# Gated DeltaNet attention, then a SwiGLU feed-forward block: batch-pair copies, a longer filler for chunk 1, and unread matrix products in the first chain

## The chip, the core and the metric

The kernel runs on one NeuronCore of a Trainium2 chip. The time is the device time of one execution in microseconds (us), the median of several runs; lower is better. TensorE is called PE in the profile (PEld for its weight loads), VectorE DVE, ScalarE ACT, GpSimd POOL and SyncE SP.

## The reference, cut to what matters

Two stages. First a delta-rule attention: for each of 4 batches and 8 heads, a 48 by 48 state is carried over 768 steps. Then all 3,072 tokens (width 384) go through a SwiGLU feed-forward block with an inner width of 1,536.

```python
k_n = k / (norm(k, axis=-1) + 1e-06)
for t in range(768):
    y[:, :, t] = q[:, :, t] @ state                 # read before the update
    v_old = k_n[:, :, t] @ state
    state += beta[t] * outer(k_n[:, :, t], v[:, :, t] - v_old)
x = y.transpose(0, 2, 1, 3).reshape(3072, 384)
g = x @ w_gate
out = (g * sigmoid(g) * (x @ w_val)) @ w_out        # weights arrive as float64
```

## The kernel before, in words

**Chunks.** The 768 steps are cut into 12 chunks of 64. A chunk holds 64 steps of all 4 batches, 256 tokens. Inside a chunk the recurrence is solved as a triangular system. Two chunks form a group, and the inverse of a group's triangular matrix is made on DVE by 31 steps of substitution (`substitute`, two instructions a step, lines 453 and 459: `tmp` and `zb`). `late_z` (486, 492) turns the result into `zt` and `d_t`. `join_late` then puts the two halves of a chunk's inverse together on PE: 32 products `p_j` at line 502, a negating copy on ACT (509), 64 products `p_j` at 517, and four copies into `zt` at 527.

**A chunk's chain** is `advance(c)`, a generator in four steps: (1) `p_r` and `p_y` from the state (not for chunk 0); (2) `p_u` (654) and its copy `uu` (663); (3) the state's products `p_s` (683) and `p_y` (671), with three copies into `y` (702, 704); (4) the transpose `p_f` (714) and the copy `x_ffn` (715). For chunk 0 the state's products come in step 4.

**The feed-forward part** of a chunk is six calls of `gate_val`, each for 256 of the 1,536 inner columns (24 PE passes: `p_gate`, `p_val`; then `sil` on ACT and the product `h_f` on DVE, line 745), and two calls of `output` (12 products `p_o` each). Chunks 0 and 1 are interleaved: three `gate_val` of chunk 0, three of chunk 1, then alternating.

**What sets the order.** Everything stands in program order, written out by hand, in one `manual_schedule`; each engine takes its instructions in that order. Between the PE blocks stand two hooks: `point(c)` emits one step of chunk c's chain or of the preparation of later chunks (`prep_step`: joins, and `products`, the transposes 377 and Gram products 389 of a later chunk's K and Q), and `fill(n)` emits DVE work: first the conversion of the float64 weights to float32 (`convert`, 36 pieces, lines 200 to 250, with an ACT instruction at 208), and when they are done, steps of the next group's inverse (`invert`). `invert` for groups from 2 on first transposes `a_sb` into `mb` (420, 423), then has POOL take a power of its diagonal (544), then scales (551, 553, 554, 323, 438, 440), then substitutes.

**PSUM** is held under four tags: `px` and `py` of two banks each, and `ffn` with four single banks. A tile with a tag waits until the readers of the tile that held it before are done.

**Before the first chunk** the beta values are fetched by 16 small DMAs on POOL's queue (331), K's norms are taken (307, 315 on DVE, 319 on POOL) and `first_betas` (340 to 344, 323) divides by them.

Of the kernel before, what the change touches and what calls it, by code (L numbers as in the profile page):

```python
# [8 lines left out]
FP32 = mybir.dt.float32  # L9
# [5 lines left out]
C = 64  # L15
DP = 64
R = 32
# [4 lines left out]
def kernel(  # L22
# [25 lines left out]
    nc = tc.nc  # L48
# [21 lines left out]
    def ps_pair(name, tag):  # L70

        return psum.tile([128, 2, 512], FP32, name=name, tag=tag, bufs=1)
# [215 lines left out]
    def half_of(x):  # L288
        return slice(64 * x, 64 * x + 64)
# [31 lines left out]
    def divide_beta(g, r_n):  # L321
        for _ in range(2):
            nc.vector.tensor_tensor(
                out=beta_b[:, g], in0=beta_b[:, g], in1=r_n, op=ALU.mult
            )
# [9 lines left out]
            ],  # L335
        )

    def first_betas():
        n = n_t[0].rearrange("p c h -> p (c h)")
        nc.vector.tensor_scalar_add(n, n, 1e-6)  # L340
        r_n = work.tile([128, R], FP32, name="r_n", tag="n_b", bufs=1)
        nc.vector.reciprocal(r_n, n)
        r_b = work.tile([128, R], FP32, name="r_b", tag="nb", bufs=1)
        nc.vector.transpose(r_b, r_n)
        divide_beta(0, r_b)

    def scale_v_heads(c):
        r = vin[c].rearrange("p par bp j d -> p (par bp j) d")
# [8 lines left out]
    def banks(name, tag):  # L357

        if tag == "ffn":
            return [ps_ffn([128, 512], name) for _ in range(2)]  # L360
        p = ps_pair(name, tag)
        return [p[:, 0], p[:, 1]]

    def turned(c, of_q, tag=None):

# [82 lines left out]
    def substitute(mb, zb):  # L448
        for j in range(R - 1):
# [14 lines left out]
            )  # L464
            yield

    QUADS = [(slice(R * n, R * n + R), R * (n % 2)) for n in range(4)]
    z_late = {}

# [22 lines left out]
        nc.vector.transpose(z_late[g], zb)  # L492
        yield

    def join_late(g, c, tags, split=False):

        zt, a, d_t = ztp[g % ZB], a_sb[g], z_late[g]
        p_j = banks("p_j", tags[0])[0].rearrange("p (h i) -> p h i", i=R)
        for h in range(HH):
            for s in range(2):  # L500
                hi, lo = QUADS[2 * s][0], QUADS[2 * s + 1][0]
                nc.tensor.matmul(p_j[hi, h], a[lo, c, h, 0:R], zt[lo, c, h, R:C])  # L502
        t2 = work.tile([128, HH, R], FP32, name="t2", tag="tmp", bufs=1)
        for s in range(2):
            hi = QUADS[2 * s][0]
            if s and split:
                nc.vector.tensor_scalar_mul(t2[hi], p_j[hi], -1.0)
            else:
                nc.scalar.mul(t2[hi], p_j[hi], -1.0)
        yield  # L510
        p_j = [p.rearrange("p (h i) -> p h i", i=C) for p in banks("p_j", tags[1])]
        n_h = HH // 2
        for of_d in (True, False):
            for h in range(HH):
                for s in range(2):
                    hi = QUADS[2 * s][0]
                    nc.tensor.matmul(  # L517
                        p_j[h // n_h][hi, h % n_h, 0:R] if of_d
                        else p_j[h // n_h][hi, h % n_h, R:C],
                        d_t[hi, :, HH * c + h],  # L520
                        ident[hi, hi] if of_d else t2[hi, h],
                    )
        copies = nc.scalar.copy, nc.vector.tensor_copy if split else nc.scalar.copy
        for s, copy in enumerate(copies):
            hi = QUADS[2 * s][0]
            for n in range(2):
                copy(zt[hi, c, n * n_h : (n + 1) * n_h], p_j[n][hi])
        yield

    def invert(g):  # L530
# [84 lines left out]
            )  # L615
        yield

    def recur(p):
        return p[:, :, 0 : NB * NJ * D].rearrange("p x (bp j d) -> p x bp j d", bp=NB, j=NJ)

    def advance(c):

        kn = knp[c % AHEAD]
# [2 lines left out]
        if c > 0:  # L626
            scale_v(c)
        r = vin.pop(c)
        p_y = recur(ps_pair("p_y", "py"))
        if c > 0:  # L630
            p_r = recur(ps_pair("p_r", "px"))
            for bp, j, par, b, first in every():
# [27 lines left out]
                skip_group_check=True,  # L660
            )
        uu = work.tile([128, 2, NB, NJ, D], FP32, name="uu", tag="r", bufs=3)
        nc.scalar.copy(uu, p_u)
        if c + 2 < NCH:
            load_v(c + 2)
        yield
# [30 lines left out]

        if 0 < c < NCH - 1:
            of_state()
        p_of_u()  # L700
        y = work.tile([128, NB, NJ, 2, D], FP32, name="y", tag="r", bufs=3)
        nc.scalar.copy(y[:, :, :, 0], p_y[:, 0])
        for b in range(2):
            nc.scalar.copy(y[half_of(b), :, :, 1], p_y[half_of(1 - b), 1])
        yield

        y_f = y.rearrange("p bp j par d -> p bp (j par d)")
# [3 lines left out]
        for bp in range(NB):  # L711
            for t in range(KT):
                at = slice(t * 128, (t + 1) * 128)
                nc.tensor.transpose(p_f[:, t, bp], y_f[:, bp, at], ident)  # L714
        nc.scalar.copy(xts[c].rearrange("p t (bp n) -> p t bp n", bp=NB), p_f)
        if c == 0:
            of_state()
        yield

    out_v = out.rearrange("(b s) d -> b s d", s=S)  # L720

# [66 lines left out]
    def steps(kind, *args):  # L788
        return gens.get((kind, args), (None, 0))[1]
# [39 lines left out]
    def prep_step(c):  # L829
# [11 lines left out]
        if going:  # L841
            next(going.pop())
            return True
        if not q_of or steps("advance", q_of[0] - 1) < 3:
            return False
        k_c, q_c = None, q_of.pop(0)
        if k_of and steps("advance", k_of[0] - AHEAD) >= 4:
            k_c = k_of.pop(0)
        gen = products(k_c, q_c)
# [45 lines left out]
    with tc.manual_schedule(  # L895
# [9 lines left out]
        for at in range(8):  # L905
            load_beta(at)
        norms(0)
        for at in range(8, 12):
            load_beta(at)

        nc.vector.memset(places[0][:, 0:1], 0)
        norms(1)
        for at in range(12, 16):
            load_beta(at)
        for n in range(4):
            stage(n)
# [8 lines left out]
        stage(11)  # L925
        copy_a, copy_v = nc.scalar.copy, nc.vector.tensor_copy
        turned(0, False)
        gram(0, False)
        turned(1, False, "py")
        gram(1, False, "py", (copy_a, copy_v))  # L930
        mb = new_mb()
        a_v = a_sb[0].rearrange("p c h i -> p i (c h)")
# [6 lines left out]
        for n in range(12, 17):  # L939
            stage(n)  # L940
        load_v(1)
        first_betas()
        zb = scale_m(mb, [(slice(0, R), mb)], beta_b[:, 0])
        nc.gpsimd.memset(ztp[0], 0.0)

# [7 lines left out]
        for n, _ in enumerate(substitute(mb, zb)):  # L953
            if n == R // 2:
                for i in range(4):
                    power_step(i)
        m_1 = turned_m(1, "ffn")
        scale_v_heads(0)
        turned(1, True, "px")
        for _ in late_z(0, zb):  # L960
            pass
        mb = new_mb()
        mbs.append(mb)
        first_join = join_late(0, 0, ("px", "py"))
        next(first_join)
        converts(2)
        next(first_join)
        nc.scalar.copy(mb[:, m_1[0][0]], m_1[0][1])
        next(first_q)
        step("advance", advance, 0)  # L970
        converts(2)
        step("advance", advance, 0)
# [6 lines left out]
        second_inverse.append(invert(1))  # L979
        next(second_inverse[0])  # L980
        second = join_late(0, 1, ("ffn", "py"))
        next(second)
        converts(2)

        def second_join():
            next(second)
            gens["join", (0,)] = [None, 2]
            gram(1, True)

        first.append(second_join)  # L990


        pairs = [(0, 0), (0, 2), (0, 4)] + [(1, 0), (1, 2), (1, 4)]
        pairs += [(c, f) for f in range(6, FT, 2) for c in range(2)]
        for c, f in pairs:
            if c == 1 and f == 0:
                finish(1)
            elif f > 0:
                point(1 if c == 0 and f < 6 else 2)
            need((6, 12, 18, 18, 24, 24)[f // 2])  # L1000
            gate_val(c, f, fill, 1 if c == 0 and f < 6 else None)
        need(len(pieces))
        for bp in range(NB):
            point(2)
            output(0, bp, fill)
        hold.clear()
        for bp in range(NB):
            point(2)
            output(1, bp, fill)
        finish(2)  # L1010
        for c in range(2, NCH):
# [37 lines left out]
```

## Time and profile before

| | us |
|---|---|
| median of 3 runs | 792.59 (791.41 to 794.15) |
| the profiled execution's own time | 788.7 |
| its span, first to last instruction | 786.7 |
| PE busy | 737.0 (94% of the span) |
| DVE busy | 403.8 (51%) |
| ACT busy | 163.6 (21%) |
| POOL busy | 67.9 (9%) |
| mean granted PE clock | 0.964 |

The table is read stage by stage. From about 210 us to the end PE hardly stops; the idle time of PE lies in the first 210 us, and so does the time at a reduced clock. In those first 180 us DVE is busy almost throughout, with the first inverse, the weights' conversion and the second inverse.

### The profile page before, as it was taken

Reading aid. Unit: us, or ns where it says so; the run is one execution under the profiler, and the core shown is the slowest. Engines: PE = TensorE matmul, PEld = TensorE weight load, DVE = VectorE, ACT = ScalarE, POOL = GpSimd, SP = SyncE. Lnnn points to the kernel's source line nnn. Section 1 sums busy time; section 2 is a strip of 40 time slices with the busy share of each in tenths; the row PEclk is TensorE's granted clock in tenths of the full one; section 3 lists DMA queues with packets and bytes.
Section 4 is the critical chain, followed back from the end, with each engine's and each line's share of the span. In section 5 each row is a group of like instructions: output and inputs, shape, how many; then the busy total and the mean of one; then the engine's idle time right before and its main releaser. Section 6 shows DMA issues by size and latency. Waiting matters only on the chain.

```text
span 786.7 us, 21538 instructions
## 1 busy us (share of the span) xinstructions
PE 737.0 (94%) x9800; PEld 588.2 (75%) x9800; DVE 403.8 (51%) x814; ACT 163.6 (21%) x296; POOL 67.9 (9%) x52
## 2 busy tenths in 40 slices
PE   5638899997999999999999999999999999999997
PEld 4537788855788688688688688688688688687784
DVE  5999699994127873067842068832068822021010
ACT  2246243201221211212111112111212111111110
POOL 9106000100003000012000021000020000000000
PEclk9856899998999999999999999999999999999999
DMA  8874244200211200312101112101101000000000
GB/s 149 205 189 116 88 108 137 61 20 12 53 22 23 45 17 3 61 23 42 32 12 19 39 28 43 31 13 23 26 17 22 21 2 2 21 2 1 21 1 20
DMA packets 86683, 34.77 MB, mean 44 GB/s; under 512 B 78848, under 2 KB 81920, under 8 KB 86592
## 3 DMA queue, kind: packets, MB, share of 16 engines
q1 hardware_dynamic: 79872, 27.93, 15.8%
q10 hardware_dynamic: 5952, 5.12, 2.9%
q8 instruction: 77, 1.26, 0.7%
q0 software_dynamic: 768, 0.35, 0.3%
q14 instruction: 14, 0.11, 0.0%
HBM read 28.66 MB, written 4.72 MB: 42 GB/s over the span
## 4 chain that ended last, share of the span: by engine, by line
PE 89%; DVE 5%; ACT 1%; issue 1%; POOL 1%; DMA 1%; ACTq 0%; DVEq 0%
PE p_gate L731 25%; PE p_o L754 24%; PE p_val L731 24%; PE p_g L389 3%; PE p_t L377 2%; PE p_j L517 2%; PE p_u L654 2%; PE p_s L683 2%; PE p_y L671 2%; DVE zb L459 1%; DVE tmp L453 1%; PE p_r L633 1%; PE p_y L642 1%; PE p_f L714 1%; POOL n_t L319 1%
## 5 line engine op out<-in xcount | busy, mean ns | idle before, releaser
L731 PE MATMUL p_gate<-x_ffn,wg_sb 128*128 128x256 f32 x864 | 203.9, 386 | 0.0
L731 PE MATMUL p_val<-x_ffn,wv_sb 128*128 128x256 f32 x864 | 199.3, 381 | 0.0
L754 PE MATMUL p_o<-wo_sb,h_f 128*128 128x384 f32 x576 | 192.4, 491 | 0.0
L731 PEld LDWEIGHTS p_val<-x_ffn,wv_sb 128*128 128x128 f32 x864 | 164.7, 191 | 22.4
L745 DVE TENSOR_TENSOR h_f<-sil,p_val 128x512 f32<-128x512 f32 x72 | 49.3, 685 | 257.1 <-PE p_val L731 256.6
L731 PEld LDWEIGHTS p_gate<-x_ffn,wg_sb 128*128 128x128 f32 x864 | 161.2, 191 | 23.0
L754 PEld LDWEIGHTS p_o<-wo_sb,h_f 128*128 128x128 f32 x576 | 108.7, 192 | 71.8 <-issue 1.4
L740 ACT ACTIVATE sil<-p_gate 128x512 f32<-128x512 f32 x72 | 43.0, 597 | 217.4 <-PE p_gate L731 188.4
L544 POOL TENSOR_TENSOR n_b<-mb,half 128x32 f32<-128x32 f32 x5 | 39.4, 7874 | 441.0 <-DVE mb L423 403.1
L459 DVE TENSOR_TENSOR zb<-zb,tmp 128x31 f32<-128x31 f32 (+15 forms) x186 | 63.7, 343 | 6.4
L453 DVE TENSOR_TENSOR tmp<-zb,mb 128x31 f32<-128x31 f32 (+15 forms) x186 | 63.6, 342 | 5.6
L762 ACT COPY o_sb<-p_o 128x384 f32<-128x384 f32 x24 | 11.5, 478 | 172.0 <-PE p_o L754 165.5
L208 ACT ACTIVATE h_f<-h_f,rebias 128x256 int32<-128x256 uint32 (+2 forms) x36 | 21.0, 612 | 47.0 <-DVE h_f L200 47.0
L692 DVE TENSOR_TENSOR state<-state,p_s 128x768 f32<-128x768 f32 x10 | 9.5, 951 | 26.1 <-PE p_s L683 26.1
L377 PE MATMUL p_t<-ident,kn 128*128 128x128 f32 x96 | 16.8, 324 | 6.5 <-DMA kn<-in_k_dram 5.7
L502 PE MATMUL p_j<-zt,a_sb 32*32 32x32 f32 x256 | 6.2, 214 | 17.3 <-DVE zt L486 11.1
L423 DVE STREAM_TRANSPOSE mb<-a_sb 32x1024 f32<-32x1024 f32 x10 | 21.3, 2135 | 0.3
L377 PEld LDWEIGHTS p_t<-ident,kn 128*128 128x128 f32 x96 | 13.3, 166 | 9.8 <-POOL mask_q L273 4.5
L402 DVE TENSOR_TENSOR p_sb<-p_g,mask_q 128x512 f32<-128x512 f32 x24 | 15.4, 684 | 8.4 <-PE p_g L389 8.4
L389 PEld LDWEIGHTS p_g<-kt 64*64 64x64 f32 x768 | 13.9, 149 | 7.7 <-issue 4.2
L502 PEld LDWEIGHTS p_j<-zt,a_sb 32*32 32x32 f32 x256 | 5.8, 129 | 18.5 <-issue 18.4
L389 PE MATMUL p_g<-kt 64*64 64x64 f32 x768 | 15.5, 236 | 3.7 <-ACT kt L379 2.3
(120 smaller groups left out, 583.9 us busy)
## 6 DMA issues: line engine op xcount, KB each, us to landing
qpad<-in_q_dram SPq DMA_DIRECT2D x48, 96.0 KB, 3.0
vin<-in_v_dram SPq DMA_DIRECT2D x96, 48.0 KB, 2.5
out_dram<-o_sb ACTq DMA_DIRECT2D x48, 96.0 KB, 2.2
kn<-in_k_dram SPq DMA_DIRECT2D x44, 96.0 KB, 3.7
zt<-in_moe_w_out_dram SPq DMA_DIRECT2D x6, 384.0 KB, 3.1
staged<-in_moe_w_out_dram SPq DMA_DIRECT2D x6, 384.0 KB, 3.1
wo_sb<-in_moe_w_gate_dram SPq DMA_DIRECT2D x4, 512.0 KB, 5.5
wo_sb<-in_moe_w_val_dram SPq DMA_DIRECT2D x4, 512.0 KB, 6.9
```

The source lines that it names most:

```text
L208: nc.scalar.activation(power.bitcast(I32), power, ACTF.Relu, bias=rebias, scale=8.0)
L377: nc.tensor.transpose(p_t[bp][:, at], x[:, bp, 2 * j : 2 * j + 2], ident)
L389: nc.tensor.matmul(p_v[par][half_of(b if of_q else b ^ par), bp, j], kt[c][half_of(par), bp, j, b], xt[half_of(par), bp, j, b],)
L423: nc.vector.transpose(out(rows, 0), in_(rows, 0))
L453: nc.vector.tensor_tensor(out=t_v, in0=zb[:, 0 : j + 1, j : j + 1].to_broadcast([128, j + 1, m]), in1=mb[:, j : j + 1, j + 1 : R].to_broad ...
L459: nc.vector.tensor_tensor(out=zb[:, 0 : j + 1, j + 1 : R], in0=zb[:, 0 : j + 1, j + 1 : R], in1=t_v, op=ALU.add,)
L517: nc.tensor.matmul(p_j[h // n_h][hi, h % n_h, 0:R] if of_d else p_j[h // n_h][hi, h % n_h, R:C], d_t[hi, :, HH * c + h], ident[hi, hi] if ...
L544: nc.gpsimd.tensor_tensor(out=n, in0=mb.rearrange("p j i -> p (j i)")[:, 0 : R * R : R + 1], in1=half, op=ALU.pow,)
L731: nc.tensor.matmul(ps[name][:, i], w_sb[:, t, (f + i) * 128 : (f + i + 1) * 128], xts[c][:, t], start=(t == 0), stop=(t == KT - 1),)
L740: nc.scalar.activation(sil, ps[name], ACTF.Silu)
L745: nc.vector.tensor_tensor(out=hs[c, f], in0=sil, in1=ps["p_val"], op=ALU.mult)
L754: nc.tensor.matmul(p_o, hs[c, f - f % 2][:, f % 2, bp * 128 : (bp + 1) * 128], wo_sb[:, f], start=(f == 0), stop=(f == FT - 1),)
```

## The change

1. **The start.** `first_betas` is split: the part that does not need beta (`first_n`: add, reciprocal, transpose) moves ahead of the last Gram copy; only `divide_beta` stays in place. All eight remaining beta DMAs are issued after the second norm's power. K of chunk 1 is transposed before the Gram products of chunk 0.
2. **Batch pairs.** In chunk 0's chain the copies `uu`, `y` and `x_ffn` are made for one pair of batches at a time: two, six and two instructions in place of one, three and one. `join_late` copies into `zt` by batch pairs also (four copies of 512 elements, as before), with its PSUM tile laid out to match.
3. **Unread products.** `keep_awake` issues products of the identity with K of chunk 0 whose result nothing reads: five of 128x512 in the gap of the first inverse (released by a memset on DVE, ten steps before the substitution's end), one of 128x512 between the two halves of the first join, one of 128x512 ahead of `p_u`, one of 128x256 ahead of `p_y` and one of 128x512 ahead of `p_f`.
4. **The order of chunks 0 and 1.** Four `gate_val` of chunk 0, then four of chunk 1, then alternating. Chunk 0's first `gate_val` no longer waits behind the state's products and the second join; these become hooks inside it. K of chunk 4 may be prepared without a Q; so K of chunk 4 is transposed during chunk 0's third `gate_val`, and K of chunk 5 goes with Q of chunk 2 during chunk 1's first two. The hook ahead of chunk 1's first `output` is dropped.

The line numbers of the changed kernel are higher by 8 to 30.

```diff
-    def first_betas():
+    def first_n():
         ...
         nc.vector.transpose(r_b, r_n)
-        divide_beta(0, r_b)
+        return r_b
...
+    def keep_awake(p, n):
+        moving = knp[0].rearrange("p bp h d -> p (bp h d)")
+        for i in range(n):
+            nc.tensor.matmul(p, ident, moving[:, 0 : p.shape[-1]], start=True, stop=True)
...
-    def join_late(g, c, tags, split=False):
+    def join_late(g, c, tags, split=False, awake=False):
...
+        p_j = ps_pair("p_j", tags[1])
+        if awake:
+            keep_awake(p_j[:, 0], 1)
...
-            for n in range(2):
-                copy(zt[hi, c, n * n_h : (n + 1) * n_h], p_j[n][hi])
+        for bp in range(NB):
+            for s, copy in enumerate(copies):
+                hi = QUADS[2 * s][0]
+                copy(
+                    zt_v[hi, :, bp].rearrange("p par j i -> p par (j i)"),
+                    p_j[hi, :, bp].rearrange("p par j i -> p par (j i)"),
+                )
...
-        p_y = recur(ps_pair("p_y", "py"))
+        p_y2 = ps_pair("p_y", "py")
+        if c == 0:
+            keep_awake(p_y2[:, 0], 1)
+        p_y = recur(p_y2)
...
-        nc.scalar.copy(uu, p_u)
+        each = range(NB) if c == 0 else (slice(0, NB),)
+        for bp in each:
+            nc.scalar.copy(uu[:, :, bp], p_u[:, :, bp])
...
+        if c == 0:
+            keep_awake(p_y2[:, 0, 0:256], 1)
         p_of_u()
+        if c == 0:
+            keep_awake(ps_pair("p_w", "px")[:, 0], 1)
...
-        nc.scalar.copy(y[:, :, :, 0], p_y[:, 0])
-        for b in range(2):
-            nc.scalar.copy(y[half_of(b), :, :, 1], p_y[half_of(1 - b), 1])
+        for bp in each:
+            nc.scalar.copy(y[:, bp, :, 0], p_y[:, 0, bp])
+            for b in range(2):
+                nc.scalar.copy(y[half_of(b), bp, :, 1], p_y[half_of(1 - b), 1, bp])
...
-        nc.scalar.copy(xts[c].rearrange("p t (bp n) -> p t bp n", bp=NB), p_f)
+        for bp in each:
+            nc.scalar.copy(x_v[:, :, bp], p_f[:, :, bp])
+        yield
         if c == 0:
             of_state()
-        yield
+            yield
...
-        if not q_of or steps("advance", q_of[0] - 1) < 3:
+        if q_of and steps("advance", q_of[0] - 1) >= 3:
+            q_c = q_of.pop(0)
+        elif not (hold and k_of and steps("advance", k_of[0] - AHEAD) >= 4):
             return False
...
         turned(0, False)
+        turned(1, False, "py")
         gram(0, False)
-        turned(1, False, "py")
+        r_b = first_n()
         gram(1, False, "py", (copy_a, copy_v))
...
+            if n == R - 11:
+                nc.vector.memset(awake, 0.0)
...
+        p_w = ps_pair("p_w", "py")
+        nc.tensor.matmul(p_w[0:1, 1, 0:1], awake, ident[:, 0:1], start=True, stop=True)
+        keep_awake(p_w[:, 0], 5)
...
-        next(second)
         converts(2)
+        def state_and_join():
+            step("advance", advance, 0)
+            next(second)
...
-            gram(1, True)
-        first.append(second_join)
+        first.extend((state_and_join, second_join, lambda: gram(1, True)))
...
-        pairs = [(0, 0), (0, 2), (0, 4)] + [(1, 0), (1, 2), (1, 4)]
-        pairs += [(c, f) for f in range(6, FT, 2) for c in range(2)]
+        pairs = [(c, f) for c in range(2) for f in range(0, 8, 2)]
+        pairs += [(c, f) for f in range(8, FT, 2) for c in range(2)]
...
         for bp in range(NB):
-            point(2)
+            if bp > 0:
+                point(2)
             output(1, bp, fill)
```

## The prediction, made before the changed kernel ran

> **What bounds the kernel now.** I read the page's engine shares first, then the chain that ended last, PE's waits, the granted clock in 1 us windows, and last the timelines of DVE, ACT and POOL.
>
> ```profile
> PE 737.0 (94%) x9800; PEld 588.2 (75%) x9800; DVE 403.8 (51%) x814; ACT 163.6 (21%) x296; POOL 67.9 (9%) x52
> PEclk9856899998999999999999999999999999999999
> ```
>
> PE is the bound, at full clock from about 220 us on. What an edit can win lies in the first 210 us: PE's idle time and its cold time. PE's waits name the idle:
>
> ```profile
> PE p_j L502 <- DVE zt L486: 11.1, 1, 11.1
> PE p_j L502 <- issue: 6.2, 1, 6.2
> PE p_g L389 <- ACT zt L527: 2.2, 1, 2.2
> ```
>
> The first is the first inverse on DVE. The second is put down to "issue", but the chain shows DVE's second inverse, whose `zt` ends at 182.34:
>
> ```profile
> 155.60 20.64 PE p_o L754 x64
> 176.24 6.20 issue
> 182.44 1.92 PE p_j L502 x64
> ```
>
> The granted clock in 1 us windows, the third figure from the right:
>
> ```profile
> 33.00:34.00 1.00, 0.72 (x52) 0.64 (x45) 0.93 (x3) 0.00 (x0) 0.00 (x0) 0.89 0.18 29
> 71.00:72.00 1.00, 1.00 (x58) 0.91 (x52) 1.00 (x5) 0.46 (x1) 1.00 (x1) 0.83 0.73 246
> 78.00:79.00 1.00, 1.00 (x41) 1.00 (x37) 0.00 (x0) 0.00 (x0) 1.00 (x1) 0.58 0.92 320
> 84.00:85.00 1.00, 1.00 (x4) 0.82 (x3) 0.72 (x2) 0.00 (x0) 0.00 (x0) 0.51 0.00 0
> ```
>
> It is 0.5 or 1.0, so each mean gives the instant: down at 33.78, up at 71.34, down at 78.16, up at 84.98. The steps are 11, 2 and 2 times 3.41 us. At 78.16 it fell although PE was 100% busy: with 32x32 products (`p_j`, 75.39 to 79.18), and 0.65 us of full-size ones before them.
>
> **What the Trainium skill says.** "TensorE: Matmul & The Clock Gate", Part 1: the clock is halved after an idle window of 3,413 ns and restored after a busy one, the windows running freely. The trace agrees, and adds that small products count as idle. The same page, Part 1 (architectural detail) and Part 3: ACT and DVE take instructions strictly in order, and matmuls never pass each other; so an unread product delays all behind it. "ScalarE: Activation LUTs", what ACT_TABLE_LOAD costs: an ACTIVATE has a fixed part (186 ns) and 0.833 ns an element. Here 384 elements take 0.48 and 768 take 0.80: 0.83 ns an element and 0.16 fixed. So 192 elements cost 0.33 (estimate), and halving a copy adds about 0.16.
>
> **The change, part by part** (after minus before, us).
>
> *Start: -0.65.* L340, L342 and L344 with their gaps (23.75 to 24.59) leave the path to the substitution: -0.84. They wait for POOL's second power, now directly behind the first (12.71+2.95=15.66); the last Gram copy queued behind them starts at 16.5, not 16.1, which the beta wait (0.35) nearly hides: +0.1. The eight beta DMAs behind the powers end at the same 20.1. The memset: +0.1.
>
> *The five products: 0 on the path.* PE idles 11.05 us there. Released near 44.1, at 1.72 us cold (a 128x256 product is 2 passes of 0.216 warm, so 512 is 0.86 warm), they wake the clock within two windows and end before 52.
>
> *First join and chunk 0's chain: +0.75.*
> - `p_j` L502 warm: 1.75 to 1.20: -0.55.
> - The product between the halves: +0.86.
> - L517: before 2.86 (with a 1.0 us hole) and 2.05, cold; warm it takes 1.9 a half anyway. I keep half the hole: -0.65.
> - Ahead of `p_u`: the product waits until all four `zt` copies have released `py`, and `p_u` stands behind it. Between the last product and this one lie 6.2 us of L517 and idling, more than any window in which the clock survived (75.39 to 81.38: it fell). So I take it that the clock falls once more near 58 to 61 and is back about 63: product 1.66 and `p_u` 1.85 on average, against 1.95 + 0.05: +1.5. Ends: 2.0 if warm, 4.2 if cold throughout.
> - `uu` to `p_y`: 0.81 + 2.0 before; 0.48 and 1.05 after, the 256 product hidden: -1.3. The first `uu` copy waits for all of `p_u`, so only the copy is halved.
> - `y`: on ACT stand `mb` L973 (0.59) and two L208 (0.92) ahead of it. Before, 0.79 of idling followed them; now PE is ahead of ACT and waits 0.8. Then six copies of 0.33 for three of 0.49: +1.3. `p_f` needs all six; the product ahead of it is hidden.
> - `p_f` warm: -0.67. `x_ffn`, two copies, 1.0, stood beside `p_s` and `p_j` (3.02, cold); now PE waits for it, then does those two in 2.25: +0.25.
>
> Sum -0.55+0.86-0.65+1.5-1.3+1.3-0.67+0.25 = +0.74.
>
> *Second join: -3.1.* Before, after L517:
>
> ```profile
> 79.20 1.05 ACT zt L527 x2
> 80.27 1.07 ACT zt L527 x2
> 81.38 1.99 PE p_g L389 x64
> 83.37 3.62 PE p_val L731 x12
> ```
>
> A `p_gate` now covers the 2.2 us; with `p_g` at 1.05 and `p_val` at 2.6 this is -4.15. L517's 3.8 us still stand alone between feed-forward products: a window fits into it in some 6 of 10 phases, and costs 1.7: +1.0.
>
> *Chunk 1's chain: +3.1.* Two waits before (`vin` 0.71, `uu` 0.33) go: -1.0. New ones, following each engine's queue: Gram of chunk 4 behind its `kt` copies, behind an L208: 0.35; `p_u` for `vin` (L355, L650 queued behind a conversion): 0.65; and steps 3 and 4 now come in `finish(1)` with no filler: `y` behind an L208 0.7 and its copies 1.5, `x_ffn` 0.9. Sum +4.1. Before, three `gate_val` covered these, the last one the copies. Chunk 5's transposes and Grams (1.84) come here from 225 to 234 us: nothing in the sum. Its K, issued on SP behind eight `vin` loads, lands near 113.5 and is needed at 115: hidden, up to 1.6 if it took the slowest K load's 6.1.
>
> *Up to the second inverse: -0.8.* Its release is the last `h_f`, which waited behind L440 (155.33 to 156.47); DVE is ahead now.
>
> *Chunk 5 early: +3.5.* Group 2's inverse starts as soon as K of 5 is there, so DVE's queue after `d_t` holds: `mb` transposes (2.13, 4.2), the wait for POOL's power, the scaling, two steps, and only then `vin` L355 and L650, for which `p_u` of chunk 2 waits. The same work later in the trace of before:
>
> ```profile
> 240.63 2.16 DVE L423 STREAM_TRANSPOSE mb<-a_sb 32x1024 f32<-32x1024 f32 x1
> ...
> 249.12 0.90 DVE L551 TENSOR_SCALAR n_b<-n_b 128x32 f32<-128x32 f32 x1 [4.27 <-POOL n_b L544]
> ...
> 251.35 1.23 DVE L440 TENSOR_TENSOR mb<-mb,nb 128x1024 f32<-128x1024 f32 x1
> ```
>
> From the transposes' end to L440's end: 9.8. Counted from the start of `p_j`: transposes end at +8.2, L440 at +18.0, steps 1.0, `vin` 2.05: +21.05. PE arrives at +17.6 (`p_j` 1.92, `p_o` 4.3, L517 3.75, `p_o` 2.78, `p_r` and `p_y` 2.0, `p_o` 2.78). So 3.5 of new waiting.
>
> *Dropped hook:* it emitted nothing on PE's path; 0. Afterwards PE has the same work as before: 0.
>
> Sum: -0.65+0.74-3.1+3.1-0.8+3.5 = **+2.8**. On the profiled execution 788.7 becomes 791.5; that one lies 3.9 below the median of the runs, so on the median it is 792.6 + 2.8 = **795.4**. A measurement tells some 0.3% (2.4 us) from no change, so this is just slower.
>
> **The rivals.**
> 1. *The clock holds (same).* If one product of 0.86 in a window is enough and the second L517 falls well, the +1.5 becomes 0 and the +1.0 goes: 2.8-2.5 = +0.3, 792.9. For it: it survived 187.4 to 190.8 with 1.26 us of `p_o` in the window. Against: it fell with 0.65, and from 54 to 60.5 there is nothing full-size.
> 2. *Faster.* The clock holds and `p_u` of chunk 2 does not wait: 0.3-3.5 = -3.2, 789.4. Its place is DVE's queue at the second inverse; it decides if POOL's 6.21 us power starts over 3.5 us earlier against PE, or PE is later. For it: PE would be later by as much as a cold clock adds. Against: the order of both queues is fixed.
> 3. *The unread products don't wake the clock (slower).* Then the first join and chain run cold: `p_j` +0.55, the product ahead of L517 +0.86, `p_u` and its product +0.7, `p_y` +0.9, `p_f` +0.7, less what ACT's queue hides, about +3: 798.4. Against: full-size products for 8 us.
>
> **How the numbers follow.** Forecast 0.42; rival 1 0.32, rival 2 0.18, rival 3 0.08. The first is slower by over 0.3% in most of its width (K of chunk 5 late, the hole in L517 0 to 1 us, clock phase 1.7), and so is rival 3; rival 1 is within. Slower 0.48, same 0.32, faster 0.20. The range 788.8 to 798.6 takes in rival 2 and most of rival 3; the slower forecast's own is 793.5 to 798.
>
> **What would show it.** Right: full clock at 52 us, half clock near 60; the `y` copies starting after L208; PE waiting about 2.5 us around `p_f` of chunk 1; `p_u` of chunk 2 waiting 3.5 us for DVE `vin`; the `p_j` of the second inverse near 182 to 184. Wrong: full clock without a break from 50 to 110 us, or no wait at that `p_u`.

## The result, and the profile after

| | before | after |
|---|---|---|
| median, us | 793.37 (791.41 to 794.15) | 797.75 (796.99 to 799.78) |
| ratio, 95% interval | 1 | 1.0063 [1.0034, 1.0092] |
| the profiled execution's own time, us | 788.7 | 798.41 |
| its span, us | 786.7 | 796.3 |

The changed kernel is slower by 0.6%, 2.4 us above the forecast of 795.4 and inside its range. The two profiled executions are 9.7 us apart, the medians 4.4; why they differ is told at the end of the next section.

The page of the changed kernel, engine shares and granted clock:

```profile
PE 748.4 (94%) x9820; PEld 590.8 (74%) x9820; DVE 403.9 (51%) x815; ACT 164.0 (21%) x301; POOL 66.3 (8%) x52
...
PEclk9677989998979999999999999999999999999999
```

PE is busy 11.4 us longer, which is about what the unread products take: 6.13 in the gap of the first inverse and 5.53 in the chain. PE's waits (total, times, longest):

```profile
PE p_j L514 <- issue: 6.2, 1, 6.2
...
PE p_f L739 <- ACT y L729: 5.0, 3, 2.3
...
PE p_u L672 <- DVE vin L668: 3.3, 2, 2.6
...
PE p_j L514 <- DVE zt L498: 1.7, 1, 1.7
```

The gap of the first inverse is filled (11.1 us of waiting became 1.7 at `p_j` and 2.7 at the releasing product). The 6.2 us ahead of the second inverse's `p_j` stayed to the tenth, but it stands elsewhere: that `p_j` starts at 189.69, where it was 182.44. DVE releases it, so the next question is what held DVE back. Its waits from the first join's `p_j` to this one, before:

```profile
DVE p_sb L402 <- PE p_g L389: 6.2, 1, 6.2
DVE h_f L745 <- PE p_val L731: 3.8, 3, 2.4
DVE h_f L241 <- ACT h_f L208: 0.4, 1, 0.4
```

and after:

```profile
DVE h_f L773 <- PE p_val L759: 18.3, 7, 7.3
```

DVE waits 7.9 us longer, and its second inverse is about that much later, less the 0.5 us by which it began earlier (first substitution step at 26.07, before 26.59). All of the waits after are for PE's `p_val`. DVE's timeline shows where the longest of them lies:

```profile
111.79 0.95 DVE L712 TENSOR_TENSOR state<-state,p_s 128x768 f32<-128x768 f32 x1
112.66 0.42 DVE L220 TENSOR_SCALAR wg_sb<-staged 128x512 uint32<-128x512 uint32 x1
...
114.71 0.69 DVE L250 SCALAR_TENSOR_TENSOR wg_sb<-wg_sb,h_f 128x512 f32<-128x512 f32 x1
122.75 0.69 DVE L773 TENSOR_TENSOR h_f<-sil,p_val 128x512 f32<-128x512 f32 x1 [7.35 <-PE p_val L759]
```

After one weight conversion (112.66 to 115.4) the next instruction in DVE's queue is the first `h_f` of chunk 1, whose `p_val` ends only at 122.7. Before, the last steps of chunk 1's chain had three `gate_val` around them, each of which hands DVE conversions; now they stand in `finish(1)`, which hands it none. PE's timeline for the same stretch:

```profile
109.25 1.11 PE L691 MATMUL p_y<-uu,p_sb 64*64 64x48 f32 x64
112.69 1.54 PE L739 MATMUL p_f<-ident,y 128*128 128x128 f32 x6 [2.33 <-ACT y L729]
115.12 4.93 PE L759 MATMUL p_gate<-x_ffn,wg_sb 128*128 128x256 f32 x12 [0.89 <-ACT x_ffn L742]
119.89 2.75 PE L759 MATMUL p_val<-x_ffn,wv_sb 128*128 128x256 f32 x12
```

The two waits were forecast (2.2 and 0.9). What came with them was not: PE's clock falls there. The windows (third figure from the right is the clock) give 112.52 and 119.36, two steps of 3.41 us apart (down, then up again):

```profile
112.00:113.00 1.00, 0.31 (x2) 0.31 (x3) 1.00 (x2) 0.63 (x2) 0.00 (x0) 0.76 0.11 15
119.00:120.00 1.00, 1.00 (x5) 0.83 (x5) 0.00 (x0) 0.00 (x0) 0.00 (x0) 0.82 0.00 0
```

`p_gate` takes 4.93 instead of 2.86 and `p_f` 1.54 instead of 0.87: 2.7 us, all of it inside DVE's wait.

**Which engine leads.** That DVE waits does not yet make it the bound: it waits for PE. Look at the tenth `gate_val` of the two chunks, before (PE, then the `h_f` on DVE):

```profile
142.49 2.75 PE L731 MATMUL p_val<-x_ffn,wv_sb 128*128 128x256 f32 x12
...
155.44 20.80 PE L754 MATMUL p_o<-wo_sb,h_f 128*128 128x384 f32 x64
182.44 1.92 PE L502 MATMUL p_j<-zt,a_sb 32*32 32x32 f32 x64 [6.20 <-issue]
```

```profile
145.35 0.69 DVE L745 TENSOR_TENSOR h_f<-sil,p_val 128x512 f32<-128x512 f32 x1
```

and after:

```profile
149.76 2.75 PE L759 MATMUL p_val<-x_ffn,wv_sb 128*128 128x256 f32 x12
...
162.71 20.80 PE L782 MATMUL p_o<-wo_sb,h_f 128*128 128x384 f32 x64
189.69 1.92 PE L514 MATMUL p_j<-zt,a_sb 32*32 32x32 f32 x64 [6.18 <-issue]
```

```profile
152.62 0.69 DVE L773 TENSOR_TENSOR h_f<-sil,p_val 128x512 f32<-128x512 f32 x1
```

In both, `h_f` starts 0.11 us after its `p_val` ends (145.24 and 152.51), with DVE free for 0.1 us before it, too short to be listed as a wait. In the changed kernel each of the first ten `h_f` starts so; before, eight of the twelve do. PE meanwhile has no wait that the profile lists: in the changed kernel from chunk 1's `x_ffn` on, in the kernel before from 97 us on. So PE's path, with its own waits for ACT and DVE, leads up to the tenth `gate_val`. From there DVE has 37.1 us of work of its own up to `p_j`, in both kernels, and `p_j` stands 27.0 us behind the start of PE's `p_o`, in both. What moved is PE's arrival at `p_o`: 162.71 instead of 155.44, +7.27. DVE's longer waits are how it follows.

PE's account to `p_o`: it starts 0.52 earlier at the first `p_j`; from there it idles 10.18 us instead of 7.58 (+2.6), the unread products take 5.5, and K of chunk 5 (transposes and Gram products) some 2.0. The remaining -2.3 goes with the clock, which is halved for 17.1 us of this stretch instead of 25.4.

The other place where time is lost is behind the second inverse:

```profile
209.72 1.15 PE L672 MATMUL p_u<-vin,zt 64*64 64x48 f32 x64 [2.59 <-DVE vin L668]
...
217.35 0.87 PE L739 MATMUL p_f<-ident,y 128*128 128x128 f32 x6 [1.69 <-ACT y L729]
218.16 1.82 PE L514 MATMUL p_j<-zt,a_sb 32*32 32x32 f32 x64
219.90 5.44 PE L759 MATMUL p_gate<-x_ffn,wg_sb 128*128 128x256 f32 x12
```

The span splits without a rest at two landmarks, the second inverse's `p_j` and chunk 2's second `p_gate` (218.60 before, 231.62 after). Up to the first: +7.25. Between them: 41.93 instead of 36.16, so +5.77 (`p_u`'s wait 2.59, colder `p_j` 0.62 and `p_gate` 2.58). From the second to the end: 564.68 instead of 568.10, so -3.42: K of chunk 5 is missing here (its work, 1.84 us in the prediction's count, now stands in the first part), and the 1.6 us wait at the `p_f` of chunk 4 is gone. Sum +9.6, the difference of the spans.

### The profile page after: what moved, and what is told of

It is laid out like the page before. It is cut to its first block, busy times and chain, and to the rows that moved or that the text cites. A ratio compares the mean times of both kernels' runs of the same rounds, so it can differ in the third digit from the quotient of the medians.

```text
span 796.3 us, 21574 instructions
## 1 busy us (share of the span) xinstructions
PE 748.4 (94%) x9820; PEld 590.8 (74%) x9820; DVE 403.9 (51%) x815; ACT 164.0 (21%) x301; POOL 66.3 (8%) x52
## 4 chain that ended last, share of the span: by engine, by line
PE 83%; DVE 11%; POOL 2%; ACT 1%; issue 1%; DMA 1%; ACTq 0%; DVEq 0%
PE p_gate L759 24%; PE p_val L759 23%; PE p_o L782 20%; DVE zb L467 3%; DVE tmp L461 3%; PE p_g L397 2%; PE p_t L385 2%; PE p_u L672 2%; PE p_j L532 1%; PE p_y L691 1%; PE p_s L703 1%; PE p_r L651 1%; PE p_f L739 1%; PE p_y L660 1%; POOL n_t L319 1%
## 5 line engine op out<-in xcount | busy, mean ns | idle before, releaser
L759 PE MATMUL p_gate<-x_ffn,wg_sb 128*128 128x256 f32 x864 | 209.2, 393 | 1.8 <-ACT x_ffn L742 1.8
L759 PEld LDWEIGHTS p_gate<-x_ffn,wg_sb 128*128 128x128 f32 x864 | 163.7, 195 | 26.0 <-ACT x_ffn L742 2.5
L461 DVE TENSOR_TENSOR tmp<-zb,mb 128x31 f32<-128x31 f32 (+15 forms) x186 | 63.5, 342 | 15.9 <-PE p_j L532 10.4
L562 POOL TENSOR_TENSOR n_b<-mb,half 128x32 f32<-128x32 f32 x5 | 37.8, 7563 | 378.8 <-DVE mb L431 337.6
L668 DVE TENSOR_TENSOR vin<-vin,p_r 128x768 f32<-128x768 f32 x11 | 10.5, 954 | 23.9 <-PE p_r L651 23.0
L672 PEld LDWEIGHTS p_u<-vin,zt 64*64 64x64 f32 x768 | 13.1, 142 | 8.8 <-DVE vin L668 4.3
L385 PE MATMUL p_t<-ident,qpad 128*128 128x128 f32 x96 | 14.5, 298 | 5.2 <-DMA qpad<-in_q_dram 5.2
L683 ACT COPY uu<-p_u 128x768 f32<-128x768 f32 (+1 forms) x13 | 9.6, 749 | 40.0 <-PE p_u L672 40.0
L672 PE MATMUL p_u<-vin,zt 64*64 64x48 f32 x768 | 14.6, 227 | 3.3 <-DVE vin L668 3.3
```

The lines of the kernel that those rows point to most:

```text
L385: nc.tensor.transpose(p_t[bp][:, at], x[:, bp, 2 * j : 2 * j + 2], ident)
L461: nc.vector.tensor_tensor(out=t_v, in0=zb[:, 0 : j + 1, j : j + 1].to_broadcast([128, j + 1, m]), in1=mb[:, j : j + 1, j + 1 : R].to_broad ...
L562: nc.gpsimd.tensor_tensor(out=n, in0=mb.rearrange("p j i -> p (j i)")[:, 0 : R * R : R + 1], in1=half, op=ALU.pow,)
L672: nc.tensor.matmul(p_u[half_of(b), par, bp, j], zt[half_of(b ^ par), par, bp, j], r[half_of(b ^ par), par, bp, j], start=first, stop=True, ...
L759: nc.tensor.matmul(ps[name][:, i], w_sb[:, t, (f + i) * 128 : (f + i + 1) * 128], xts[c][:, t], start=(t == 0), stop=(t == KT - 1),)
```

## The experiments

Theory A: until the second inverse DVE is the bound, and its idle time counts one to one. The rivals: B, the unread products and halved copies cost; C, PE's own path decides, as the prediction summed it, and what DVE has in its queue does not matter. D, later, concerns the early K of chunk 5. To tell A from C, two numbers are read in each trace: when PE starts `p_o`, and how far the second `p_j` stands behind that. If DVE's queue matters, the second one changes. Every ratio is to the kernel before on the same chip, with its 95% interval.

**Part 4, the order, alone**, on the kernel before.

```diff
-        pairs = [(0, 0), (0, 2), (0, 4)] + [(1, 0), (1, 2), (1, 4)]
-        pairs += [(c, f) for f in range(6, FT, 2) for c in range(2)]
+        pairs = [(c, f) for c in range(2) for f in range(0, 8, 2)]
+        pairs += [(c, f) for f in range(8, FT, 2) for c in range(2)]
...
+        first.extend((state_and_join, second_join, lambda: gram(1, True)))
```

> The kernel before with part 4 of the change alone (four gate_val of chunk 0, then four of chunk 1; K of chunks 4 and 5 early; second join inside chunk 0's first gate_val); start, single copies and no unread products as before. Theory A (the loss is made by the new order: the last steps of chunk 1's chain stand with no gate_val and no conversion beside them, DVE idles there, and its second inverse, which PE waits for near 190 us, comes later): slower than before, 797 to 803 us, ratio 1.005 to 1.012, with a DVE wait of 5 to 8 us at the first h_f of chunk 1 and the p_j of the second inverse at 189 to 194 us. Theory B (the loss is made by the unread products and the halved copies in chunk 0's chain): within 0.3% of before. Theory C (the sum in the prediction, PE's path): terms of the order alone are -3.1+3.1-0.8+3.5=+2.7, so 796.

Measured 797.52, ratio 1.0073 [1.0050, 1.0096]; DVE waits 6.10 at the first `h_f` of chunk 1, `p_j` at 189.72. The order alone makes the whole loss, so B is out as its cause; between A and C the time does not tell, as both forecast about this. PE starts `p_o` at 162.76, and `p_j` comes 27.0 us later, as before.

**The rest without part 4.**

```diff
-        pairs = [(c, f) for c in range(2) for f in range(0, 8, 2)]
-        pairs += [(c, f) for f in range(8, FT, 2) for c in range(2)]
+        pairs = [(0, 0), (0, 2), (0, 4)] + [(1, 0), (1, 2), (1, 4)]
+        pairs += [(c, f) for f in range(6, FT, 2) for c in range(2)]
```

> The changed kernel with part 4 taken back: the order of gate_val and hooks as before, but the new start, the batch pairs and the unread products kept. Theory A (the order makes the loss): as before or a little faster, 789 to 793.5 us, ratio 0.995 to 1.000; DVE's waits up to the second inverse at most the 10.4 us of before. Theory B (unread products and halved copies make it): as the changed kernel, 796 to 799, ratio 1.004 to 1.007. Theory C (the prediction's sum): -0.65+0.74=+0.1, so 793.4, ratio 1.000.

Measured 792.01, ratio 1.0015 [1.0001, 1.0028]: start, batch pairs and unread products bring nothing that can be told. In this execution the first `p_j` comes 1.6 us earlier (51.20 instead of 52.79), but PE starts `p_o` at 155.32, practically where it did before: the chain with its 5.0 us of unread products takes the start back. DVE waits 13.0 us, so A's forecast of at most 10.4 was wrong.

**Without the unread products.**

```diff
-        if awake:
-            keep_awake(p_j[:, 0], 1)
...
-        keep_awake(p_w[:, 0], 5)
```

> The changed kernel without any unread product (the five in the gap and the four in chunk 0's chain left out, with the memset and the small product that release them); nothing that is read is left out. Theory A: chunk 0's chain runs at the halved clock, its first feed-forward block comes 1 to 3 us later, DVE waits as much longer for the first h_f, and the end comes up to 3 us later than with them: 798 to 801, ratio 1.005 to 1.010. Theory B (the unread products cost more than they bring): faster than the changed kernel by their own time on the path (some 3 us): 794 to 795, ratio 1.001 to 1.003.

Measured 797.26, ratio 1.0072 [1.0048, 1.0097], against 1.0063 with them: neither gain nor cost. Chunk 0's chain runs cold (`p_f` 1.54, first `p_gate` 5.46), but from the first `p_j` to its first `p_val` 25.36 us pass (53.11 to 78.47), where the changed kernel takes 25.45 (52.27 to 77.72): what the products win in clock they spend themselves. DVE's waits are the same to 0.1 us (18.4).

**Three conversions moved into chunk 1's last steps.** PE's work stays, DVE gets something to do: A and C forecast different times.

```diff
             while steps("advance", c) < 4:
                 step("advance", advance, c)
+                if c == 1:
+                    converts(2 if steps("advance", 1) < 4 else 1)
```

> The changed kernel with three of the 36 weight conversions moved forward on DVE: two are issued after the third step and one after the fourth step of chunk 1's chain, where DVE waits 7.35 us for the first h_f of chunk 1 in the changed kernel. PE's order and work stay. Theory A (DVE's idle time there sets when the second inverse ends): that wait falls below 1.5 us, the p_j of the second inverse comes 5 to 7 us earlier (183 to 185 us instead of 189.7), and the time is 791 to 793.5, ratio 0.997 to 1.000. Theory C (PE's own waits and cold clock in that place make the loss, as the prediction's sum has it): PE's work before 190 us is the same and its waits too, so no change: 797 to 798.5, ratio 1.005 to 1.007.

Measured 803.02, ratio 1.0153 [1.0126, 1.0179]: slower, against both theories. The trace has a part of A's forecast: `p_j` comes at 186.19, 3.5 us earlier, though PE starts `p_o` 2.3 us later (165.02); from there to `p_j` it is 21.2 us instead of 27.0. Then 45.64 us pass to chunk 2's second `p_gate` instead of 41.93. Two suspects: `x_ffn` on ACT behind the conversions' activations (PE waits 3.20 instead of 0.89), or DVE's queue after the inverse. So the conversions were put behind `x_ffn`:

```diff
+                if c == 1:
+                    converts(3) if steps("advance", 1) == 4 else None
```

> The changed kernel with three weight conversions moved forward on DVE to the end of chunk 1's chain, behind x_ffn; K of chunk 5 early as in the change. It tells why the first such version, with the conversions ahead of x_ffn, was slower (803). If the x_ffn copy, 2.3 us late behind them on ACT, was the reason: 792 to 794, ratio 0.999 to 1.003. If the reason is DVE's queue at the second inverse (the scaling of the inverse of chunks 4 and 5, which waits 4.8 us for POOL, then stands ahead of the zt copies of chunk 2's join, for which PE waits): 799 to 803, ratio 1.009 to 1.015, with PE waiting 2 to 4 us for DVE zt.

Measured 801.89, ratio 1.0126 [1.0095, 1.0157]. The wait for `x_ffn` is back at 0.89, and the kernel is still slow: mainly the queue, then. DVE's timeline of this kernel, and then PE's:

```profile
193.43 0.69 DVE L519 TENSOR_SCALAR t<-p_j 32x512 f32<-32x512 f32 x1
198.95 0.90 DVE L569 TENSOR_SCALAR n_b<-n_b 128x32 f32<-128x32 f32 x1 [4.83 <-POOL n_b L562]
...
203.50 0.69 DVE L542 COPY zt<-p_j 32x512 f32<-32x512 f32 x1
```

```profile
198.88 1.15 PE L651 MATMUL p_r<-state,kt 64*64 64x48 f32 x64
205.67 1.96 PE L660 MATMUL p_y<-state,qt 64*64 64x48 f32 x64 [5.64 <-DVE zt L542]
```

In the changed kernel the `zt` copies stand ahead of this wait for POOL (200.27 and 203.25); here they stand behind it. As the conversions end sooner, the inverse of chunks 4 and 5 is issued earlier. The early K of chunk 5 lets it start there at all, so K was made late:

```diff
-        elif not (hold and k_of and steps("advance", k_of[0] - AHEAD) >= 4):
+        elif not (hold and k_of and k_of[0] == AHEAD and steps("advance", k_of[0] - AHEAD) >= 4):
...
-        if k_of and steps("advance", k_of[0] - AHEAD) >= 4:
+        if k_of and (k_of[0] - AHEAD < 1 or q_c != 2) and steps("advance", k_of[0] - AHEAD) >= 4:
```

> The changed kernel with K of chunk 5 prepared as late as before (with Q of chunk 3 instead of Q of chunk 2), so that the inverse of chunks 4 and 5 no longer starts while chunk 2's chain runs; K of chunk 4 stays early. By the prediction's step 'chunk 5 early' (wait for vin, 2.6 us in the trace of the changed kernel, with the clock that falls behind it): the p_u of chunk 2 waits under 1 us, and the time is 2.5 to 4 us shorter, 794 to 795.5, ratio 1.001 to 1.003. If that queue on DVE costs nothing because another wait takes its place: 797 to 798.5.

Alone, measured 797.84, ratio 1.0078 [1.0053, 1.0103]: no gain, though the wait at `p_u` of chunk 2 is gone. From the second landmark to the end it has 567.8 us again, not 564.7: what the late K saves at `p_u` it gives back there.

**Both: conversions moved, K of chunk 5 late.**

> The changed kernel with K of chunk 5 late, and with three weight conversions moved forward on DVE to the end of chunk 1's chain (behind x_ffn on ACT, so that x_ffn is not delayed, as it was by 2.3 us where they stood ahead of it). Theory A (DVE's idle time ahead of the second inverse makes most of the loss, the early inverse of chunks 4 and 5 the rest): second inverse's p_j 5 us earlier than in the changed kernel, at 183 to 186, nothing on DVE ahead of its zt copies, 790 to 793, ratio 0.998 to 1.001. Theory C (PE's own waits and cold clock make it): no better than with K of chunk 5 late alone, 794 to 796.

Measured 792.83, ratio 1.0010 [0.9989, 1.0031], `p_j` at 183.20. Against the same kernel without the moved conversions this is 5.0 us in the medians, with PE's products as they were. PE starts `p_o` 1.9 us later than there (162.01, was 160.09) and still `p_j` comes 4.25 us earlier: it follows `p_o` by 21.2 us instead of 27.4. So DVE's queue matters, and C as it was put is out. Nor does A hold one to one: DVE's wait at the first `h_f` of chunk 1 fell from 7.37 to 0.14, by more than `p_j` moved. What the moved conversions shorten is DVE's work behind the last `h_f` that PE releases: that is now the twelfth, and only 20.9 us of work follow it, where in the changed kernel 37.1 us followed the tenth. The other 1.8 us of the 6.1 us between the two spans lie behind `p_j`. The queue at the second inverse was the reason that the first test failed.

**Four more unread products in chunk 1's last two steps**, on the changed kernel.

```diff
+        if c == 1:
+            keep_awake(ps_ffn([128, 512], "p_w"), 3)
         y_f = y.rearrange("p bp j par d -> p bp (j par d)")
...
+        if c == 1:
+            keep_awake(ps_ffn([128, 512], "p_w"), 1)
         x_v = xts[c].rearrange("p t (bp n) -> p t bp n", bp=NB)
```

> The changed kernel with four more unread 128x512 products in chunk 1's last two steps: three ahead of its p_f, where PE waits 2.3 us, and one ahead of the x_ffn wait, so that PE's clock does not fall there (it falls at 112.5 us in the changed kernel: p_f 1.54 instead of 0.87, the p_gate behind it 4.93 instead of 2.86). If that cold spell is on the path, through DVE's wait for the first h_f of chunk 1 or through PE: 2 to 3 us shorter, 795 to 796, ratio 1.002 to 1.004. If it is hidden (PE waits 6 us for the second inverse anyway, and DVE is not moved): 797.5 to 798.5.

Measured 796.25, ratio 1.0048 [1.0033, 1.0064]. The clock stays up, and from `p_s` to `p_val` 9.09 us pass instead of 11.61. But in the profiled execution that chain had begun 2.6 us later, so PE starts `p_o` where it did (162.78), and the second `p_j` stands where it was (189.76). The time is between the two forecasts, and its interval overlaps that of the changed kernel: the cold spell's price in time stays open.

**The inverse of chunks 4 and 5 held** until `p_u` of chunk 2 is issued; K of chunk 5 early.

```diff
-            if fills:
+            if fills and (fills[0][0] != 2 or steps("advance", 2) >= 2):
```

> The changed kernel with K of chunk 5 prepared early as it is, but DVE's inverse of chunks 4 and 5 held back until p_u of chunk 2 is issued, so that it no longer stands ahead of vin. With K of chunk 5 late, the wait of that p_u went, yet the time did not: theory D says that the early K of chunk 5 also gives back as much as the wait costs (its 1.84 us of PE work is done before the second inverse, where PE idles 6.2 us, and fills a 1.6 us wait at p_f of chunk 4). Then holding the inverse alone keeps the gain and drops the wait: 794 to 795.5, ratio 1.002 to 1.0045. If the wait at p_u only moves on to the next release: 797 to 798.5.

Measured 796.10, ratio 1.0060 [1.0038, 1.0083], above the forecast. The wait at `p_u` is gone, and the last part stays short (564.4). So D is seen in the trace, but a gain in time from holding the inverse alone can't be told from the changed kernel's 1.0063.

**The kernel before with two conversions moved** into its own 6.2 us wait.

```diff
         next(second)
         converts(2)
+        converts(2)
```

> The kernel before with two of the 36 weight conversions moved forward on DVE, into its 6.2 us wait for the second join (ahead of p_sb). PE's work stays as it is; as the conversions end sooner, the second inverse's join is issued one block of products earlier. Theory A (up to the second inverse DVE is the bound, and its idle time counts one to one): DVE's waits fall from 10.4 to some 6 us, the second inverse's p_j comes 4 to 5 us earlier (178 instead of 182.4), and the kernel is 3 to 5 us faster than before, ratio 0.994 to 0.997. Theory C (PE's path decides): within 0.3% of before.

Measured 791.00, ratio 0.9982 [0.9966, 0.9997]: just outside no change, and much less than forecast. `p_sb` waits 2.7 instead of 6.2, and the first `h_f` 3.57 instead of 2.36, as PE reached it 2.9 us later (`h_f` at 89.94 instead of 87.08): PE's wait for the join's copies on ACT grew from 2.2 to 3.7. DVE's waits sum to 10.8, `p_j` is at 181.75. This is where the two numbers are plainest: `p_j` follows `p_o` by 23.4 us instead of 27.0, but PE starts `p_o` 2.9 us later (158.30), and 0.7 us is left.

**A version from these runs**: the changed kernel with three conversions at the end of chunk 1's chain, the inverse of chunks 4 and 5 held, and the four products.

> The changed kernel with three edits that the runs point to: three weight conversions moved forward to the end of chunk 1's chain, the inverse of chunks 4 and 5 held until p_u of chunk 2, and four unread products in chunk 1's last two steps that keep PE's clock up. By theory A and D their gains add (about 5.4, 3 and 1.5 us, the first and last partly the same DVE wait): second inverse's p_j at 180 to 184 us, 788 to 791, ratio 0.994 to 0.998. If the gains share one wait: 792 to 794.

Measured 788.35, ratio 0.9962 [0.9947, 0.9976], `p_j` at 181.47. With the clock up in chunk 1's chain PE starts `p_o` at 160.29, 2.4 us earlier than in the changed kernel, and `p_j` follows by 21.2. And with two more conversions ahead of chunk 0's first `gate_val`:

```diff
         second = join_late(0, 1, ("ffn", "py"))
         converts(2)
+        converts(2)
```

> As the kernel with the three edits, and two more conversions moved forward, to ahead of chunk 0's first gate_val, where DVE waits 4.5 us for the first h_f. Theory A: 2 to 4 us faster still, 785 to 789, ratio 0.991 to 0.996. Against it: their ACT instructions stand ahead of the state copy and of the join's copies on ACT, as in the kernel before with two conversions moved, where a part of DVE's wait only moved on to the next h_f; then no better than without this edit.

Measured 782.67, ratio **0.9883 [0.9852, 0.9914]**, faster than both kernels and than was forecast. DVE's waits in this kernel between the two `p_j` (another, of 0.2, is left out):

```profile
DVE h_f L777 <- PE p_val L763: 6.0, 6, 1.8
DVE h_f L200 <- DMA staged<-in_moe_w_out_dram: 1.7, 1, 1.7
DVE h_f L200 <- DMA zt<-in_moe_w_out_dram: 0.9, 1, 0.9
```

And PE's timeline at the join:

```profile
171.68 8.23 PE L786 MATMUL p_o<-wo_sb,h_f 128*128 128x384 f32 x25
179.84 1.20 PE L514 MATMUL p_j<-zt,a_sb 32*32 32x32 f32 x64
180.97 2.85 PE L786 MATMUL p_o<-wo_sb,h_f 128*128 128x384 f32 x8
```

There is no idle time ahead of `p_j` any more: PE comes last, 18.2 us after `p_o` began. The clock, which in the kernel with three edits fell in that idle time (at 180.87), stays up, and `p_j` takes 1.20, not 1.92. That is why it won more than its 1.6 us of earlier `p_j` over that kernel (781.4 to 785.9 in the spans): the part behind it takes 36.99 instead of 39.76.

**The runs by the three parts.** From the first join's `p_j` to the start of PE's `p_o`; from there to the second inverse's `p_j`; DVE's waits in these two together, and what is left of them without the waits; then from that `p_j` to chunk 2's second `p_gate`; then to the end (us, one profiled execution each).

| kernel | PE to `p_o` | on to the second `p_j` | DVE's waits | rest | to `p_gate` | to the end |
|---|---|---|---|---|---|---|
| before | 102.7 | 27.0 | 10.4 | 119.3 | 36.16 | 568.1 |
| after | 110.4 | 27.0 | 18.3 | 119.1 | 41.93 | 564.7 |
| order alone | 110.4 | 27.0 | 18.3 | 119.1 | 42.82 | 563.5 |
| without the order | 104.1 | 27.8 | 13.0 | 118.9 | 39.02 | 568.0 |
| without unread products | 110.5 | 27.0 | 18.4 | 119.1 | 40.28 | 564.3 |
| K of 5 late | 108.5 | 27.4 | 16.9 | 118.9 | 38.01 | 567.8 |
| conversions behind `x_ffn` | 112.7 | 21.2 | 15.8 | 118.1 | 46.65 | 567.7 |
| the same, K of 5 late | 109.5 | 21.2 | 12.5 | 118.2 | 35.64 | 568.4 |
| two conversions, before | 105.9 | 23.4 | 10.8 | 118.5 | 40.05 | 568.3 |
| three edits | 107.9 | 21.2 | 11.1 | 118.0 | 39.76 | 564.7 |
| and two conversions more | 109.1 | 18.2 | 8.8 | 118.4 | 36.99 | 564.6 |

The rest column is an account and not a cause: DVE has the same work in every kernel (118 to 119 us, in the three kernels not listed too), so its waits must make up any difference, whoever causes it. The first two columns tell who does. Where no conversion is moved, the second one is 27.0 (up to 27.8 in the two kernels where DVE had waited 0.5 to 0.9 us for a DMA), and the whole loss stands in the first, PE's. Where conversions are moved, the second one falls to between 18.2 and 23.4; what they win there, less what PE's arrival loses, is the gain at `p_j`. Which part of the new order costs PE how much was tested only for K of chunk 5 (2.0 us to `p_o`); what the steps without a filler cost (waits of 2.33 and 0.89 us, and the clock that falls there) is read from the traces, not tested by itself.

The column to `p_gate` holds the luck: the kernel without part 4 has the order of before there, and takes 39.02 where before took 36.16, with two `p_o` blocks cold (5.49 and 4.44 instead of 4.37 and 2.85). The profiled execution of before lies 3.9 us under the median of its runs; this fits the gap between 9.7 in the profiles and 4.4 in the medians, though single executions don't prove it.

## Why the prediction was right, and where it was wrong

The direction and the size of the time were right, and the new order is what costs. But the sum that was written did not get there: its terms up to the second inverse come to -0.7, where the trace has +7.25. In the parts of the prediction these are -0.52, +2.9, -3.95, +8.8 and 0.0.

- **What bounds the kernel.** That PE's idle and cold time decide is right up to the tenth `gate_val`, and not from there on: 37.1 us of DVE's work then end at `p_j`. The 6.2 us in which PE waits for it were read, and even put down to DVE, but that DVE's queue could be shortened there was not asked.
- **Start, -0.65:** -0.52. **The five products, 0 on the path:** right; they ran from 44.47 to 50.60, `p_j` found a full clock.
- **First join and chunk 0's chain, +0.74:** +2.9 on PE. Three sizes were off: the hole among the join's products stayed whole (1.29 us), the clock came back near 68 and not 63, and the 256 product, called hidden, stood in front of `p_y` for 1.2. That the clock falls once more near 58 was right (57.9).
- **Second join, -3.1:** -3.95 on PE. The copies are covered, as forecast, and the clock held: the +1.0 did not come.
- **Chunk 1's chain, +3.1:** this is the term that was mis-sized most, +8.8 up to `p_o`. Each wait came within 0.15 us of the forecast (`kt` 0.50, `vin` 0.71, `y` 2.33, `x_ffn` 0.89), 3.4 more than before. Left out was the fall of the clock in the last two (2.7). K of chunk 5 (2.0) was called "nothing in the sum", which holds for the whole kernel but not up to the second inverse. Some 0.7 is left over.
- **Up to the second inverse, -0.8:** 0.0. "DVE is ahead now" was wrong: it follows PE, and the last `h_f` again starts 0.9 us behind its `p_val`. The `p_j` expected near 182 to 184 came at 189.69.
- **Chunk 5 early, +3.5:** the mechanism is as told; the wait is 2.59. PE came 17.4 us after `p_j` started, as forecast (17.6); DVE's `vin` ended at 20.0, not 21.05, since POOL's power took 5.44 us, not 6.21. The clock was low for longer behind it (3.2 more in this execution), and the 1.6 us wait at chunk 4's `p_f` went, which "afterwards 0" did not have. So the term is about +4.2 in this trace. No difference in time showed (K late: 1.0078, early: 1.0063), and in the trace with the late K the clock is low elsewhere (`p_o` behind `p_j` 5.00 and 4.06, with the early K 4.27 and 2.85).
- **Sum.** +2.8 was forecast between the profiled executions; the trace has +9.6 in the spans: 8.0 too little up to the second inverse, 1.1 too much behind it. On the medians it is 4.4, so the forecast was 2.4 low. That it came so near is in part luck: the profile that the terms were read from lies 3.9 us under its median, and what the account missed up to `p_o` is of that size and more.
- **The rivals.** A held clock (1) did not come; (2) failed with the wait at `p_u`; (3) gave 798.4, near the measured time, but its cause is excluded: the products woke the clock.

The clock gate as the Trainium skill's "TensorE: Matmul & The Clock Gate", Part 1, tells it (halved after an idle window of 3,413 ns, restored after a busy one) was used for every reading of the windows, and this trace agrees: the edges at 112.52 and 119.36 are 6.84 us apart, two windows. That "small products count as idle", as the prediction put it, is shown for the 32x32 ones alone: in the kernel before the clock rose at 71.34, at the end of a window (67.93 to 71.34) that held only the transposes `p_f` (1.54 us) and the 64x48 products `p_s` (1.96 us).

## What to carry to other kernels

Where one engine idles for another's long chain, the sum of either engine's waits closes the account and does not tell who leads. Look at each handover whether the released engine had been free, even for 0.1 us, and split the path at the last handover where it had: ahead of it the releasing engine's path counts, behind it the other's remaining work. When the order of a hand-made schedule changes, list what each engine finds in its queue in the stretches that lose their filler; moving three conversions there, with a foreign wait kept out of the queue, won 5 us by shortening that remaining work, while the nine unread products of the change brought nothing that could be told. And moving work earlier moves what stands behind it in the same queue: look at what will be issued in its old place.

## What was not expected of the hardware

- Four unread 128x512 products (3.9 us in all) inside two waits of 2.3 and 0.9 us kept the clock up and shortened the stretch by 2.5 us, although they overran the waits.
- PE stopped for 0.5 to 1.3 us in the middle of the first join's 32x32 products in all fourteen kernels, for nothing that the trace names, at a full clock (1.29 in the changed kernel) and at a halved one (0.99 in the kernel before).
- The same program part, with PE waiting for the same release, took 36.2 or 39.0 us. The clock was halved from 180.6 to 187.4 in the one, and from 180.3 to 190.6 and 194.0 to 197.4 in the other: how its windows fall over an idle stretch of 6 to 7 us is worth some 3 us.
